# A layer norm's reciprocal square root as a power on GpSimd, tile by tile, with a finer opening and a new order of the early key chunks

## The chip, the cores and the metric

The kernel runs on one core of one Trainium2 chip. The metric is device time in microseconds (us), the median of several executions. Engines by the profile's names: PE is TensorE, PEld its weight loads, DVE is VectorE, ACT is ScalarE, POOL is GpSimd. L-numbers in profile lines are lines of the kernel that was profiled, so the same statement has other numbers before and after.

Ratios are the mean time of one kernel's runs over that of the other's of the same rounds, so not quite the ratio of the medians quoted.

## The reference

One pre-norm block: attention with 32 heads of 16 on 2048 tokens of width 512, then a gated feed-forward of width 1792.

```python
def _layernorm(x, axis=-1, eps=1e-5):
    m = jnp.mean(x, axis=axis, keepdims=True)
    v = jnp.var(x, axis=axis, keepdims=True)
    return (x - m) / jnp.sqrt(v + eps)

h  = x + attention(_layernorm(x))            # q, k, v = norm(x) @ wqkv; softmax; @ wo
h2 = h + (sigmoid(n @ w_gate) * (n @ w_up)) @ w_down     # n = _layernorm(h)
```

## The kernel before

The kernel is recorded by a Python program that keeps its own clock for each engine and lays down a static order of instructions from assumed durations. The attention is 2048 units (one head, 128 keys, 512 queries). ScalarE does most of the exponentials; VectorE does the rest with integer arithmetic (a first pass named `J`, then four-unit passes named `X`). The background work (layer norm, projections, later the feed-forward) is fitted between.

A unit needs its key chunk: 512 keys, normalised, transposed, projected. At the start only chunk 0 exists, so the first units depend on how fast chunks 1 to 3 are made ready. Each group of four heads must have all its value products in one accumulator before the next group's may start, so exponentials of a later group are held in one of 44 slots.

Before, the opening took one square root for four tiles on ScalarE and projected 512 queries at once:

```python
Task(("r", 0), [("f", 0, i) for i in range(TQ)], [("A", 330, lambda: A.activation(
    out=rstds[0][:], in_=mvs[0][:, :, 1], func=ACT.Sqrt, bias=eps_t[:, 0:1]))])
Task(("i", 0), [("r", 0)], [("D", 180, lambda: V.reciprocal(...))])
# ... apply, transpose, copy per tile, then:
Task("k", es + ["w0"], [("P", 1000, lambda: proj0(0))], bank=1)     # 4 matmuls, 128x512
Task("q", es + ["w0"], [("P", 1000, lambda: proj0(1))], bank=1)
```

The later layer norms, all but the last one in the tail, used an integer first guess and two Newton steps on VectorE, eleven small operations, once for a chunk and after the last tile's statistics:

```python
def newton_jobs(dst, var, *dep, pr=0):
    ...
    def seed():                      # 3 operations
        V.tensor_scalar(out=v[:], in0=var, scalar1=1e-5, scalar2=None, op0=ALU.add)
        ...                          # shift, multiply-add on int32
    def step(out):                   # 4 operations, done twice
        V.tensor_tensor(out=t[:], in0=y[:], in1=y[:], op=ALU.mult)
        ...
def early_ln(c):
    ...                              # statistics of 4 tiles -> js
    jn = newton_jobs(rstds[c][:], mvs[c][:, :, 1], *js, pr=pr)
    for i in range(TQ):
        ja.append(dve(325, lambda i=i: apply(c, i), jn, ...))
```

The order of the first blocks, as (group, key chunk), all for query chunk 0:

```python
early = [(0, 0), (0, 1), (1, 0), (0, 2), (0, 3), (1, 1), (1, 2), (1, 3)]
```

## Time and profile before

| | before |
|---|---|
| median (range), us | 837.8 (833.7 to 838.7, 4 runs) |
| span of the profiled run, us | 836.8 |
| first exponential of the attention, us | 16.95 |
| ScalarE busy, 20 to 70 us | 27.3 of 50 |
| eleven-operation chains on VectorE | 8 |

Busy time by engine, and the group of VectorE's exponentials (count, busy us, mean ns), from the page of the kernel before:

```profile
PE 748.3 (89%) x8275; PEld 289.7 (35%) x8275; DVE 779.3 (93%) x1525; ACT 766.8 (92%) x786; POOL 2.9 (0%) x7
...
L1109 DVE TENSOR_SCALAR J<-PS 128x512 int16<-128x512 f32 x470 | 312.4, 684 | 13.6 <-PE PS L986 7.9
```

VectorE and ScalarE are both over 90% busy over the whole span, and that hides the start. The table of windows for 20 to 70 us (us from the span's start, then each engine's busy us and instruction count, then the granted clock and DMA):

```profile
core 0: us, PE busy (x) PEld busy (x) DVE busy (x) ACT busy (x) POOL busy (x), PEclk, DMA share, GB/s
20.00:30.00 10.00, 8.26 (x59) 2.87 (x58) 8.58 (x25) 6.04 (x7) 0.00 (x0) 1.00 0.01 2
30.00:40.00 10.00, 9.31 (x71) 3.25 (x70) 8.82 (x29) 10.00 (x13) 0.00 (x0) 1.00 0.00 0
40.00:50.00 10.00, 7.93 (x25) 1.76 (x24) 5.23 (x9) 4.61 (x6) 0.00 (x0) 0.62 0.00 0
50.00:60.00 10.00, 6.37 (x31) 2.46 (x30) 7.59 (x23) 2.64 (x3) 0.00 (x0) 0.67 0.09 21
60.00:70.00 10.00, 9.23 (x42) 2.24 (x40) 5.50 (x9) 4.03 (x5) 0.00 (x0) 0.68 0.47 165
```

ScalarE falls to 2.64 of 10 us, VectorE too is far from full, and the granted clock is 0.62 to 0.68 on average from 40 to 70 us. ScalarE's waits from 18 to 70 us (total us, times, longest):

```profile
ACT pt L1252 <- PE PS L986: 19.9, 9, 8.4
ACT pe L1252 <- PE PS L986: 2.7, 1, 2.7
```

So 22.6 us are waits for scores. The longest, 8.4 us, stands behind this stretch of VectorE's timeline (start, us, instruction), the chain for chunk 3:

```profile
53.68 0.16 DVE L657 TENSOR_SCALAR nv<-mv 128x4 f32<-128x4 f32 x1
...
55.67 0.16 DVE L668 TENSOR_TENSOR rstd<-ny,nt 128x4 f32<-128x4 f32 x1
55.87 0.41 DVE L334 TENSOR_SCALAR xn_551<-xb_111,mv,rstd 128x512 bf16<-128x512 bf16 x1
```

Eleven operations take 53.68 to 55.87, and only then can the first of four tiles be applied. In the opening (timeline of all engines):

```profile
1.25 2.26 POOL L235 MEMSET Vaug<- 128x512 bf16 x1
...
1.54 2.01 DVE L240 TENSOR_SCALAR ident_76<-ident_bf 128x128 bf16<-128x128 bf16 x1
...
9.64 0.41 DVE L334 TENSOR_SCALAR xn_179<-xb_108,mv,rstd 128x512 bf16<-128x512 bf16 x1
...
12.86 2.98 PE L347 MATMUL PS<-xnT_80,w_114 128*128 128x512 bf16 x8 [0.61 <-DVE xnT_80 L341]
...
16.95 1.94 ACT L1252 ACTIVATE pt<-PS 128x1024 f16<-128x1024 f32 x2 [0.48 <-PE PS L986]
```

The first apply starts at 9.64 us, and the eight projections take 2.98 us. The doubling of a 128x128 identity takes 2.01 us; it ends with GpSimd's memset.

### The profile page before, as it was taken

How to read it: one execution, taken by the hardware profiler on the slowest of the kernel's cores; microseconds unless marked ns; L12 is line 12 of the kernel's file. 1: busy time of each engine (PE TensorE's matmuls, PEld its weight loads, DVE VectorE, ACT ScalarE, POOL GpSimd, SP SyncE). 2: the span in 40 equal slices, each digit the busy share in tenths (PEclk: the TensorE clock that was granted, in tenths of full speed). 3: DMA queues.
4: the chain of work that ended last, by engine and by line, in shares of the span. 5: the costliest groups of instructions: out<-in, count | busy, mean ns of one | idle time of the engine just before them, and what ended most of it. 6: DMA issues, size and time to landing. Idle time of an engine off the chain costs nothing.

```text
span 836.8 us, 19835 instructions
## 1 busy us (share of the span) xinstructions
PE 748.3 (89%) x8275; PEld 289.7 (35%) x8275; DVE 779.3 (93%) x1525; ACT 766.8 (92%) x786; POOL 2.9 (0%) x7
## 2 busy tenths in 40 slices
PE   4879988888989989999998999899989999989987
PEld 1322222222222232222233334333444454344444
DVE  6858999999999999999999999999998999999963
ACT  5728999999999999999899999998998999989952
POOL 1000000000000000000000000000000000000000
PEclk9959999999999999999999999999997999999999
DMA  6010000200000001021000021010211133013050
GB/s 213 1 59 30 1 1 1 65 1 1 2 1 2 14 1 51 26 64 51 20 20 3 27 65 52 27 33 14 71 52 52 40 105 100 14 32 98 8 183 16
DMA packets 53055, 33.83 MB, mean 40 GB/s; under 512 B 3040, under 2 KB 52960, under 8 KB 52960
## 3 DMA queue, kind: packets, MB, share of 16 engines
q1 hardware_dynamic: 51328, 31.33, 12.4%
q8 instruction: 66, 1.08, 0.5%
q10 hardware_dynamic: 1632, 1.18, 0.4%
q14 instruction: 29, 0.24, 0.1%
HBM read 30.41 MB, written 2.10 MB: 39 GB/s over the span
## 4 chain that ended last, share of the span: by engine, by line
ACT 39%; PE 27%; DVE 25%; issue 8%; DMA 1%; SPq 0%; ACTq 0%; DVEq 0%
ACT pt L1252 35%; DVE J L1109 9%; PE PS L986 8%; PE PS L754 5%; PE PS L735 5%; PE PS L1086 4%; DVE X L1143 4%; ACT pe L1252 2%; DVE hT L807 2%; DVE X L1133 2%; ACT th L765 2%; PE PS L270 1%; DVE X L1138 1%; DVE Vaug L274 1%; DVE xs L1034 1%
## 5 line engine op out<-in xcount | busy, mean ns | idle before, releaser
L1252 ACT ACTIVATE pt<-PS 128x1024 f16<-128x1024 f32 (+2 forms) x661 | 706.9, 1253 | 33.8 <-PE PS L986 22.3
L1109 DVE TENSOR_SCALAR J<-PS 128x512 int16<-128x512 f32 x470 | 312.4, 684 | 13.6 <-PE PS L986 7.9
L1086 PE MATMUL PS<-pt,Vaug 128*17 128x256 f16 (+1 forms) x2300 | 176.1, 310 | 1.4 <-DVE xs L1034 0.8
L1143 DVE TENSOR_TENSOR X<-J,X 128x1024 f16<-128x1024 f16 (+1 forms) x244 | 155.9, 665 | 0.0
L1086 PE MATMUL PS<-X,Vaug 128*17 128x256 f16 (+1 forms) x1410 | 139.0, 312 | 4.2 <-DVE X L1133 2.8
L1086 PEld LDWEIGHTS <-Vaug 128*17 128x17 bf16 x3777 | 84.0, 90 | 106.4 <-issue 96.7
L1138 DVE TENSOR_SCALAR X<-J 128x2048 int16<-128x2048 int16 (+2 forms) x127 | 82.0, 645 | 0.1
L1133 DVE TENSOR_SCALAR X<-J 128x2048 int16<-128x2048 int16 (+2 forms) x127 | 82.0, 645 | 0.0
L735 PE MATMUL PS<-xnT_80,wgu 128*128 128x256 bf16 (+1 forms) x336 | 63.5, 320 | 0.9 <-DVE hT L807 0.2
L735 PEld LDWEIGHTS <-wgu 128*128 128x128 bf16 x560 | 46.3, 99 | 45.4 <-issue 30.9
L754 PE MATMUL PS<-wd,hT 128*128 128x512 bf16 x196 | 55.1, 383 | 0.0
L986 PEld LDWEIGHTS <-KT_84 32*128 32x128 bf16 x768 | 23.6, 92 | 80.5 <-issue 74.6
L986 PEld LDWEIGHTS <-KT_85 32*128 32x128 bf16 x768 | 24.9, 92 | 70.7 <-issue 68.7
L549 PE MATMUL PS<-wo_sb 128*128 128x512 bf16 x143 | 47.8, 386 | 0.2 <-DVE KT_85 L630 0.2
L765 ACT ACTIVATE th<-PS 128x512 f32<-128x512 f32 (+1 forms) x63 | 41.0, 651 | 7.4 <-DVE hT L748 7.1
L986 PEld LDWEIGHTS <-KT_86 32*128 32x128 bf16 x768 | 24.4, 91 | 65.5 <-issue 64.2
L986 PE MATMUL PS<-QT_90,KT_85 32*128 32x256 bf16 (+1 forms) x384 | 36.6, 315 | 10.6 <-ACT pt L1252 9.3
L986 PEld LDWEIGHTS <-KT_87 32*128 32x128 bf16 x768 | 23.1, 91 | 63.6 <-issue 62.8
L986 PE MATMUL PS<-QT_91,KT_85 32*128 32x256 bf16 (+1 forms) x384 | 35.9, 312 | 9.0 <-ACT pt L1252 8.1
L986 PE MATMUL PS<-QT_95,KT_87 32*128 32x256 bf16 (+1 forms) x384 | 36.6, 308 | 5.6 <-ACT pt L1252 5.0
L986 PE MATMUL PS<-QT_94,KT_87 32*128 32x256 bf16 (+1 forms) x384 | 36.8, 308 | 4.9 <-ACT pt L1252 4.1
L986 PE MATMUL PS<-QT_92,KT_86 32*128 32x256 bf16 (+1 forms) x384 | 35.5, 308 | 6.3 <-ACT pt L1252 6.0
(209 smaller groups left out, 644.2 us busy)
## 6 DMA issues: line engine op xcount, KB each, us to landing
wgu<-in_B_w_gate_dram SPq DMA_DIRECT2D x35, 256.0 KB, 2.9
wgu<-in_B_w_up_dram SPq DMA_DIRECT2D x35, 256.0 KB, 3.2
out_dram<-ob SPq DMA_DIRECT2D x16, 128.0 KB, 1.7
wd<-in_B_w_down_dram SPq DMA_DIRECT2D x1, 1792.0 KB, 7.3
xr<-in_A_x_dram SPq DMA_DIRECT2D x14, 128.0 KB, 3.3
X<-in_B_w_gate_dram SPq DMA_DIRECT2D x3, 512.0 KB, 3.8
X<-in_B_w_up_dram SPq DMA_DIRECT2D x3, 512.0 KB, 4.8
wv_sb<-in_A_wqkv_dram SPq DMA_DIRECT2D x1, 512.0 KB, 6.8
```

The lines of the kernel that those rows point to most:

```text
L549: nc.tensor.matmul(PS[:, 1 + (st["ring"] + 1) % st["R"], :], lhsT=wo_sb[:, 0, 0:P], rhs=wo_sb[:, 0, :], start=True, stop=True)
L735: nc.tensor.matmul(ps[:, 0:CW[qc]], lhsT=w[:, d, :], rhs=HN[qc][:, d, cols(qc)], start=(d == 0), stop=(d == DC - 1))
L754: nc.tensor.matmul(ps, lhsT=hT[:, f, q:q + P], rhs=wd[:, f, :], start=(f == 0), stop=(f == FC - 1))
L765: nc.scalar.activation(out=th[:, 0:ps.shape[-1]], in_=ps, func=ACT.Tanh, scale=0.5)
L807: nc.vector.scalar_tensor_tensor(out=hT[:, f:f + k, cols(qc)], in0=th[f][:].rearrange("p (k n) -> p k n", k=k), scalar=1.0, in1=ps2.rearra ...
L986: nc.tensor.matmul(pss[:, ui, i * CW[qc]:(i + 1) * CW[qc]], lhsT=KT[g // 2][32 * j:32 * j + 32, k * P:(k + 1) * P], rhs=q[32 * j:32 * j + ...
L1086: nc.tensor.matmul(acc[32 * j:32 * j + VW, 0:w], lhsT=Vaug[:, kt * SPAN[qc] + i, h, :], rhs=un.ap[:, i * w:(i + 1) * w], start=(c + i == 0 ...
L1109: nc.vector.tensor_scalar(out=J[:, k, :], in0=src, scalar1=ZOFF, scalar2=0.0, op0=ALU.add, op1=ALU.max)
L1133: V.tensor_scalar(out=X[:, 0, 0:k, :], in0=J[:, 0:k, :], scalar1=POWER, scalar2=LITTLE, op0=ALU.bitwise_and, op1=ALU.bitwise_or)
L1138: V.tensor_scalar(out=X[:, 1, 0:k, :], in0=J[:, 0:k, :], scalar1=FRACTION, scalar2=HALF, op0=ALU.bitwise_and, op1=ALU.bitwise_or)
L1143: V.tensor_tensor(out=x, in0=J[:, a:b, :].bitcast(FP16), in1=x, op=ALU.mult)
L1252: ex = nc.scalar.activation(out=pt, in_=pss[:, 0:wa, :], func=ACT.Exp, scale=AS)
```

## The change

The intent: take the small chains off VectorE and let each tile go on alone; load one activation table in place of two; project 128 queries at a time, with matmuls that nobody reads keeping TensorE's clock up; and give ScalarE two groups' units for every key chunk that is ready. The core of the diff:

```diff
+    def rstd_of(dst, var, eps=1e-5):
+        v = small.tile([P, 1], FP32, name="nv")
+        nc.gpsimd.tensor_scalar(out=v[:], in0=var, scalar1=eps, scalar2=None, op0=ALU.add)
+        nc.gpsimd.tensor_tensor(out=dst, in0=v[:], in1=power[:], op=ALU.pow)
...
-    nc.gpsimd.memset(Vaug[:, :, :, DH:VW], 0.5)      # was right after make_identity
-    nc.vector.tensor_scalar(out=ident2[:], in0=ident_bf[:], scalar1=2.0, ...)   # now at the end
+    nc.scalar.activation(out=A0[:], in_=eps_t[:], func=ACT.Exp)
...
-    Task("k", es + ["w0"], [("P", 1000, lambda: proj0(0))], bank=1)
+        Task(("r", 0, i), [("f", 0, i)], [("G", 750, lambda i=i: rstd_of(...))])
+        Task(("a", 0, i), [("r", 0, i)], [("D", 340, lambda i=i: apply(0, i))])
+        for w in (1, 0):
+            Task(("p", w, i), [("e", 0, i), "w0"], [("P", 340, lambda w=w, i=i: proj0(w, i))], ...)
...
+    def keep_warm(until):
+        ...
+            E.matmul(PS[:, 4, :], lhsT=fill[:, 0:P], rhs=fill[:], start=True, stop=True)
...
+    nc.gpsimd.memset(Vaug[:, :, :, DH:VW], 0.5)      # now after the opening's four powers
...
-        jn = newton_jobs(rstds[c][:], mvs[c][:, :, 1], *js, pr=pr)
+            j = rstd_job(rstds[c][:, i:i + 1], mvs[c][:, i, 1:2], j)      # one for each tile
...
-    early = [(0, 0), (0, 1), (1, 0), (0, 2), (0, 3), (1, 1), (1, 2), (1, 3)]
+    early = [(0, 0), (1, 0), (0, 1), (1, 1), (0, 2), (0, 3), (1, 2), (1, 3)]
...
         if st["R"] > 1 and wide["i"] == 0 and late(st["R"] - 1):
+            while st["open"] is not None:       # a guard: no ring place is given up half used
+                flush()
+                try_bg(1e9, 1e12)
```

The later layer norm (`wo_ln`) uses the same power for each tile.

## The prediction

> **What bounds the kernel now.** In the long middle the exponentials do: in the table of windows ScalarE is busy 19.8 to 20.0 us of nearly every 20 us between 70 and 380 us, VectorE 19.7 to 20.0; the page gives ScalarE 92%, VectorE 93%. Around 400 to 420 and 560 to 600 us TensorE is full (up to 20.0 of 20) and ScalarE falls to 18.2 to 18.9. The start is different. In the timeline the first exponential starts at 16.95 us; ScalarE then waits 4.0 us for scores of key chunk 1 (24.4 to 28.4), and from 40 to 70 us it is busy only 11.3 of 30 us, VectorE 18.3 of 30, with the granted clock at 0.50 for most of 43 to 66 us. The longest wait there (view of waits) is 8.4 us for scores, behind the layer norm of chunk 3: eleven tiny VectorE operations, 53.7 to 55.9, then apply, transposes, projection. So before 70 us about 40 us of ScalarE time is not exponentials.
>
> **What the change does, costed.**
> 1. Opening. Today ScalarE issues loads to 4.6 us, loads the square-root table (1.28 us), ends its second statistics pass at 9.2, then takes one square root for all four tiles; VectorE applies from 9.64; the projections run eight 128x512 matmuls in 2.98 us (about 0.43 us apart, against 0.22 later). The change loads the exponential table at once, drops the second table load, lets each tile go on alone and projects 128 queries at a time at a warmed clock. The Trainium skill, "TensorE: Matmul & The Clock Gate", Part 1, says that about 3.4 us of sustained work lifts the halved clock; the 0.43 and 0.22 us spacings agree. Leaving out the doubling of the identity also frees VectorE: 2.01 us today, overlapping GpSimd's 2.26 us memset. I estimate the first exponential at 10.5 us: 6 us earlier.
> 2. Reciprocal square roots. Eight chains of eleven operations, 2.2 us each, leave VectorE: 17.5 us. GpSimd gets 26 pairs of tiny instructions, which no view of before times; the schedule assumes 0.8 us a pair. An exponential costs ScalarE about 0.45 us (706.9 us over 1,578 units) and VectorE about 1.36; rebalancing 17.5 us is worth 17.5 x 0.45/1.81, about 4 us.
> 3. Order. Two groups' units on chunk 0 give ScalarE 32 units, about 15 us, before it needs chunk 1. VectorE needs about 9 us for each chunk's preparation without the chain. The waits at 24 and 40 to 70 us should largely go; they hold about 22 us of ScalarE, 12 us of VectorE. If half is recovered, about 10 us. Held exponentials fill 32 of 44 slots, and the forced flushes may take some back.
>
> These sit on the early critical path; ScalarE-bound work afterwards should move forward as a block. The tail from 800 us stays.
>
> **Prediction.** 837.8 - 6 - 4 - 10 = 818 us; 8 in 10: 804 to 831. Faster over 2%: 0.62; within 2%: 0.35; slower: 0.03.
>
> **What would show it.** First exponential at 9.5 to 12 us; ScalarE over 20 of 30 us busy from 40 to 70; no chains of tiny VectorE operations; GpSimd busy about 20 to 30 us; VectorE exponentials up by about 10 from 470; matmuls of the opening near 0.22 us per 512 columns.
>
> **What would make it wrong.** The powers take far over 0.8 us and the in-order VectorE stands in front of apply. The skill, "GPSIMD Engine Reference", section 1, says the two share SBUF interfaces; the 2.01 us operation beside the memset fits. Or slots run out and ScalarE waits for value products; or low TensorE activity still halves the clock at 40 to 66 us, or somewhere new; or the time won early is lost at TensorE-bound stages, leaving 8 to 12 us.

## The result, and the profile after

The changed kernel takes 812.49 us (811.89 to 812.93, 4 runs) against 837.84 us (4 runs) for the kernel before; ratio 0.971, 95% interval 0.968 to 0.974. The profiled spans are 810.3 and 836.8 us: 26.5 us less.

The same page lines, changed kernel:

```profile
PE 737.8 (91%) x8279; PEld 291.4 (36%) x8279; DVE 767.4 (95%) x1437; ACT 761.7 (94%) x779; POOL 31.1 (4%) x67
...
L1134 DVE TENSOR_SCALAR J<-PS 128x512 int16<-128x512 f32 x472 | 312.5, 683 | 8.5 <-PE PS L1011 2.1
```

The chains are gone and GpSimd works 31.1 us, but VectorE's exponentials are 472, where they were 470. The same windows:

```profile
core 0: us, PE busy (x) PEld busy (x) DVE busy (x) ACT busy (x) POOL busy (x), PEclk, DMA share, GB/s
20.00:30.00 10.00, 9.43 (x73) 3.33 (x71) 9.81 (x24) 9.84 (x12) 5.02 (x12) 1.00 0.01 2
30.00:40.00 10.00, 10.00 (x63) 3.27 (x61) 9.69 (x22) 9.58 (x12) 2.37 (x6) 1.00 0.01 2
40.00:50.00 10.00, 9.74 (x73) 3.01 (x73) 9.49 (x19) 9.65 (x10) 0.79 (x2) 1.00 0.04 5
50.00:60.00 10.00, 8.16 (x53) 2.41 (x53) 7.68 (x15) 6.77 (x8) 0.00 (x0) 1.00 0.55 180
60.00:70.00 10.00, 9.73 (x107) 2.64 (x108) 9.68 (x18) 9.64 (x10) 0.00 (x0) 1.00 0.01 2
```

ScalarE is busy 45.5 of 50 us, and the clock is full from 20 to 70 us. Its waits from 18 to 70 us:

```profile
ACT pt L1280 <- PE PS L1011: 3.1, 4, 2.6
ACT pe L1280 <- PE PS L1011: 1.0, 3, 0.5
ACT pe L1280 <- PE PS L1111: 0.4, 1, 0.4
```

They are 4.5 us in place of 22.6. The opening, however, is barely shorter (timeline):

```profile
6.09 0.38 DVE L349 TENSOR_SCALAR xn_182<-xb_110,mv,rstd 128x512 bf16<-128x512 bf16 x1
...
6.39 0.41 DVE L349 TENSOR_SCALAR xn_184<-xb_110,mv,rstd 128x512 bf16<-128x512 bf16 x1
...
7.73 2.26 POOL L468 MEMSET Vaug<- 128x512 bf16 x1
...
7.81 2.33 DVE L349 TENSOR_SCALAR xn_219<-xb_110,mv,rstd 128x512 bf16<-128x512 bf16 x1 [0.46 <-POOL rstd L260]
...
15.24 2.93 ACT L1280 ACTIVATE pt<-PS 128x1024 f16<-128x1024 f32 x3
```

The first exponential comes at 15.24 us. One apply took 0.41 us, the fourth 2.33; it ends just after GpSimd's memset does (7.73 + 2.26 = 9.99 us). The chain of waits of the changed kernel (start, us, what) shows what else stood in the way:

```profile
4.31 0.23 POOL nv L259
...
7.19 0.60 POOL rstd L260
...
7.81 0.24 DVE xn_219 L349
8.05 2.02 issue
```

The chain runs through GpSimd from the first pair at 4.31 us to the fourth power: four pairs, one after the other, 3.5 us. Then come 0.24 us of the apply and 2.02 us called "issue": this profile shows no event for what held the apply, so the part of it that nothing explains is put there.

**Where the time came from.** A landmark that both kernels pass in the same order is the transposition of a finished group's accumulator (48 in all, read from the timelines). The third starts at 122.2 us before and at 102.5 after: 19.7 us ahead. The lead is 16.3 us at the 32nd (612.6 and 596.3), and 26.1 at the last (804.9 and 778.8). One landmark is not a fine measure: the lead at the first four is 16.7, 21.0, 19.7 and 16.4 us. So 16 to 20 us come from the first 100 us or so, nothing clear is won over the next 500, and the rest is won after 600 us.

### The profile page after: what moved, and what is told of

Its sections match the earlier page's. It is cut to its first block, busy times and chain, and to the rows that moved or that the text cites. A ratio compares the mean times of both kernels' runs of the same rounds, so it can differ in the third digit from the quotient of the medians.

```text
span 810.3 us, 19793 instructions
## 1 busy us (share of the span) xinstructions
PE 737.8 (91%) x8279; PEld 291.4 (36%) x8279; DVE 767.4 (95%) x1437; ACT 761.7 (94%) x779; POOL 31.1 (4%) x67
## 4 chain that ended last, share of the span: by engine, by line
ACT 40%; DVE 25%; PE 23%; issue 10%; POOL 1%; DMA 0%; DVEq 0%; ACTq 0%
ACT pt L1280 36%; DVE J L1134 10%; PE PS L1011 7%; DVE X L1168 5%; PE PS L1111 4%; PE PS L779 4%; PE PS L760 4%; ACT pe L1280 3%; DVE X L1158 2%; DVE hT L832 2%; DVE X L1163 2%; PE PS L284 1%; ACT th L790 1%; DVE xs L1059 1%; PE PS L1418 1%
## 5 line engine op out<-in xcount | busy, mean ns | idle before, releaser
L1280 ACT ACTIVATE pt<-PS 128x1024 f16<-128x1024 f32 (+2 forms) x649 | 689.3, 1238 | 12.5 <-PE PS L1111 6.8
L1163 DVE TENSOR_SCALAR X<-J 128x2048 int16<-128x2048 int16 (+3 forms) x125 | 81.8, 655 | 0.0
L1158 DVE TENSOR_SCALAR X<-J 128x2048 int16<-128x2048 int16 (+3 forms) x125 | 81.7, 654 | 0.0
L1280 ACT ACTIVATE pe<-PS 128x1024 f16<-128x1024 f32 (+2 forms) x44 | 48.0, 1184 | 1.4 <-PE PS L1011 1.0
```

The source lines that it names most:

```text
L1158: V.tensor_scalar(out=X[:, 0, 0:k, :], in0=J[:, 0:k, :], scalar1=POWER, scalar2=LITTLE, op0=ALU.bitwise_and, op1=ALU.bitwise_or)
L1163: V.tensor_scalar(out=X[:, 1, 0:k, :], in0=J[:, 0:k, :], scalar1=FRACTION, scalar2=HALF, op0=ALU.bitwise_and, op1=ALU.bitwise_or)
L1280: ex = nc.scalar.activation(out=pt, in_=pss[:, 0:wa, :], func=ACT.Exp, scale=AS)
```

## The experiments

Three parts can be switched: the opening (O), the power on GpSimd after the opening (R), and the order with its guard (G). For reading, here are all runs in one table. "Wait" is what ScalarE's exponentials waited from 18 to 70 us, "third" the landmark named above, "rest" the span less it, "lead" how much earlier than in the kernel before the first four landmarks come, on average. The lead is the steadier of the two early measures, since each version has its own static order and single landmarks shift by some us with it. Medians are of 4 runs; the kernel before was run 7 times in each of three later sets, with medians of 837.8, 836.5 and 837.0. Each part brings its planned durations along (in R, for instance, 870 ns in place of 810 for one tile's statistics).

| kernel | first exp. | wait | lead | third | rest | span | median |
|---|---|---|---|---|---|---|---|
| before | 16.95 | 22.6 | 0 | 122.2 | 714.6 | 836.8 | 837.8 |
| O alone | 15.44 | 24.0 | -0.5 | 124.6 | 719.9 | 844.5 | 845.7 |
| R alone | 17.54 | 9.0 | 12.2 | 106.0 | 728.1 | 834.1 | 838.0 |
| G alone | 18.25 | 12.4 | 6.6 | 111.1 | 728.4 | 839.5 | 841.3 |
| O and R, mended | 15.74 | 14.0 | 4.1 | 118.3 | 714.6 | 832.9 | 834.3 |
| O and G | 14.89 | 12.9 | 7.6 | 114.6 | 717.1 | 831.7 | 836.2 |
| R and G | 17.07 | 5.3 | 17.5 | 103.3 | 717.9 | 821.2 | 822.9 |
| all: the changed kernel | 15.24 | 4.5 | 18.5 | 102.5 | 707.8 | 810.3 | 812.5 |
| all, chain in later layer norm | 15.24 | 4.5 | 18.5 | 102.5 | 719.6 | 822.1 | 823.4 |
| all, one power for a chunk | 14.98 | 7.8 | 14.2 | 109.9 | 709.4 | 819.3 | 825.8 |
| all, no unread matmuls | 15.70 | 5.8 | 16.3 | 104.5 | 706.6 | 811.1 | 813.4 |
| all, plan's latency 70 ns | 14.91 | 5.6 | 18.0 | 105.8 | 712.0 | 817.8 | 818.9 |
| all, memset first | 12.75 | 4.7 | 20.7 | 100.2 | 708.2 | 808.4 | 810.2 |

### The order alone (g_only)

```diff
-    early = [(0, 0), (0, 1), (1, 0), (0, 2), (0, 3), (1, 1), (1, 2), (1, 3)]
+    early = [(0, 0), (1, 0), (0, 1), (1, 1), (0, 2), (0, 3), (1, 2), (1, 3)]
+            while st["open"] is not None: flush(); try_bg(1e9, 1e12)
```

> The kernel before with the new order of the early blocks alone. Theory 1 (the order is the main part: two groups' units on one key chunk bridge ScalarE's wait for the next chunk): 12 to 16 us faster than before, ScalarE busy over 20 of the 30 us from 40 to 70. Theory 2 (the early hole is made by the eleven-operation chains on VectorE and the halved clock behind them; the order matters little without the power on GpSimd): under 6 us faster, ScalarE under 16 of 30 us there, and the clock still halved between 40 and 70.

Measured: 841.29 us, ratio to before 1.0045 (1.0006 to 1.0085). Theory 1 as I had put it falls: the order alone makes nothing faster. Theory 2's clock condition fails too: the low clock from 40 to 70 us shrinks to one window of 3.4 us at 48.5 us. ScalarE's waits from 18 to 70 us in this run:

```profile
ACT pt L1255 <- PE PS L986: 7.4, 6, 3.1
ACT pe L1255 <- PE PS L1086: 3.2, 2, 1.9
ACT pe L1255 <- PE PS L986: 1.8, 4, 0.9
```

They are 12.4 us, about half of what they were, and 19.8 of the 30 us from 40 to 70 are busy, between the marks of the two theories. The order does bridge part of the hole: the lead over the first four landmarks is 6.6 us. By the end it has been lost again, and why was not tested.

### The power alone (r_only)

```diff
-    jn = newton_jobs(rstds[c][:], mvs[c][:, :, 1], *js, pr=pr)
+        j = rstd_job(rstds[c][:, i:i + 1], mvs[c][:, i, 1:2], j)     # and the same in wo_ln
```

> The kernel before with the power on GpSimd in the early chunks and in the later layer norm alone. Theory 1: 3 to 5 us faster (17.5 us of VectorE work shared out), the wait for chunk 3 at 53 to 62 us stays. Theory 2: 10 us or more faster, the halved clock at 43 to 66 us gone.

Measured: 838.04 us, ratio 1.0023 (0.9975 to 1.0071): nothing. Theory 2's sign is there (no low clock in the records before 285 us; wait 9.0 us, lead 12.2 us), its time is not. The lead is given back between 106 and 430 us, in windows such as these of the same run:

```profile
280.00:300.00 20.00, 15.42 (x108) 5.25 (x108) 16.03 (x32) 14.17 (x14) 3.54 (x6) 0.74 0.00 1
380.00:400.00 20.00, 17.30 (x124) 5.27 (x124) 19.90 (x35) 15.69 (x16) 0.00 (x0) 1.00 0.11 34
```

ScalarE has 14.17 and 15.69 of 20 us there. From 100 to 430 us it waits 14.1 us in this run, 8.8 of them for value products that have to free an exponential's slot; the kernel before waits 3.2 us in that stretch. At 285.3 us the clock was halved for 10.2 us. The 10.9 us more of waits are about what the lead was. Why this static order has them there was not tested.

### The opening alone (o_only)

```diff
# the changed opening; old order, no guard; newton_jobs in early_ln and wo_ln
```

> The new opening alone (loads, one table, tile by tile, 128 queries at a time, unread matmuls, GpSimd power in the first chunk only), old order, chains on VectorE after it. Both theories: first exponential at about 15.2 us as in the changed kernel, against 16.95, so about 2 us faster in all, and no more, because the hole at 40 to 70 us stays. A result of 6 us or more would say that the opening moves the clock's low windows too.

Measured: 845.73 us, ratio 1.0108 (1.0066 to 1.0149): slower, clear of the noise though by under 2%. Neither theory expected that. The first exponential came at 15.44 us, as expected, but the hole stayed (24.0 us of waits), so the earlier start only made ScalarE wait earlier; the clock records hold half clock for 55.1 us in all, against 40.1 before. Why 8 us were lost, and not just nothing won, is not shown.

### Power and order (r_g)

> Power and order together, old opening. If the three parts add up, this is the changed kernel less 2 us: 22 to 25 us faster than before. If the new opening matters more than its 1.7 us (through the warm clock or the earlier start), it is under 20 us faster.

Measured: 822.93 us, ratio 0.983 (0.980 to 0.987), with the two edits above together. It is 14.8 us faster than before, so by the expectation's own mark (under 20 us) the opening counted for more than its 1.7 us. By the third landmark this run is within 0.8 us of the changed kernel; the other 10.1 us come later, where the two kernels have the same work.

Two parts that alone gave +0.3 and +3.5 us give -14.8 together. The table shows where this comes from, and it is not the start: the leads of R and G alone, 12.2 and 6.6 us, add up to about the 17.5 us of both. It is what follows. At the end of the span R alone is 2.7 us ahead of the kernel before and G alone 2.7 behind, so each has lost over 9 us of its lead; both together are 15.6 ahead and have lost 1.9. So these three runs don't show that the two parts need each other in the first 100 us; they show that each alone loses its lead later, for a reason that stays open.

### Without the order: a wrong result (o_r), and mended (o_r_mended)

> The changed kernel with the old order of early blocks. So far: order alone 841.3, power alone 838.0, opening alone 845.7, power and order 822.9, all three 812.5. Theory A (order and power need each other: the order gives ScalarE 32 units to chew, the power makes VectorE deliver the next chunk before they are eaten, so either alone leaves the hole): 830 to 838, with ScalarE idle for 8 us or more in 20 to 50 us. Theory B (each part's worth is only the luck of the static plan that the recording makes): anything from 812 to 845, unrelated to the early idle time.

This version was the changed kernel with the old order and without the guard. It gave a wrong result (relative error 0.24; 834.78 us), which shows what the guard is for; its time is not used. The two single-part runs without the guard (R alone and O alone) were correct.

```diff
-    early = [(0, 0), (1, 0), (0, 1), (1, 1), (0, 2), (0, 3), (1, 2), (1, 3)]
+    early = [(0, 0), (0, 1), (1, 0), (0, 2), (0, 3), (1, 1), (1, 2), (1, 3)]
     # the guard stays
```

> The run without the new order once more, with the guard that keeps a ring place from being given up while a background item is half done in it (its absence gave the wrong result). Theory A (order and power need each other) expects 830 to 838 us again and ScalarE idle for 8 us or more between 20 and 50 us; if the wrong run's time was an artefact of its wrong plan, 812 to 822.

Measured: 834.30 us, ratio 0.9955 (0.991 to 1.000), correct, 14.0 us of waits. The time is where theory A put it: without the order, the power and the opening are worth under 1%. The other sign is weaker than expected: ScalarE was idle for 6.5 us between 20 and 50 us, not for 8 or more. The lead is 4.1 us.

### Without the power (o_g)

```diff
-            j = rstd_job(rstds[c][:, i:i + 1], mvs[c][:, i, 1:2], j)
+        jn = newton_jobs(rstds[c][:], mvs[c][:, :, 1], *js, pr=pr)           # and in wo_ln
```

> The changed kernel with the eleven-operation chain on VectorE again in the early chunks and in the later layer norm (the power stays in the first chunk). Theory A: 830 to 840, the wait for chunk 3 near 45 to 60 us is back as in the run of the order alone (ScalarE busy under 15 of 20 us there). Theory B: no relation.

Measured: 836.23 us, ratio 1.0003 (0.998 to 1.003), waits 12.9 us. The time is again where theory A put it: the order and the opening without the power are worth nothing. ScalarE was busy 11.8 of 20 us from 40 to 60, as expected. The lead is 7.6 us. With the new opening, then, the two parts do need each other at the start: with one of them the lead is 4.1 or 7.6 us, with both 18.5.

### The chain back in the later layer norm alone (wo_newton)

```diff
-            jr.append(rstd_job(rstd[:, i:i + 1], mv[:, i, 1:2], j))
+        jn = newton_jobs(rstd[:, 0:n], mv[:, 0:n, 1], j)
```

> The changed kernel with the chain back in the later layer norm alone; early chunks keep the power. If freeing VectorE in the long middle is worth what the prediction says (five chains of 2.2 us, 11 us of VectorE, times 0.25), 814 to 817 us; if the middle gives nothing (its landmarks showed none between 100 and 600 us), 811 to 814; over 820 would say that the later chains cost more than their VectorE time, through low clock windows.

Measured: 823.38 us, ratio 0.984 (0.982 to 0.987). It equals the changed kernel within 0.1 us for the first ten landmarks (up to 254 us), is then up to 5.6 us ahead of it (at 382 us), and after that falls behind, to 10.3 us at the last. That is more than either of my smaller figures. Low clock does not explain it: the clock is at half for 10.2 us from 428 us, where the changed kernel has 3.4 us, but over the whole span it is at half for 18.6 us, less than the changed kernel's 20.7. Read this one with the run after next.

### One power for a whole chunk (pool_whole)

```diff
-            j = rstd_job(rstds[c][:, i:i + 1], mvs[c][:, i, 1:2], j)         # each tile
+        j = rstd_job(rstds[c][:], mvs[c][:, :, 1], *ja)                      # after the last tile
```

> The changed kernel with the power still on GpSimd, but after the opening one pair of instructions for a whole chunk after its last statistics, instead of one pair for each tile. It takes as much off VectorE as the change does. If the worth of the power is that it frees VectorE, 811 to 816 us; if it is that each tile's apply and transposes go on alone, without waiting for the last tile's statistics, 820 us or more, with waits of ScalarE for scores back between 25 and 60 us.

Measured: 825.77 us (820.2 to 831.7), ratio 0.989 (0.982 to 0.996). Two runs lie near 821 us and two near 831, the latter at a mean clock of 0.967 and 0.971 against 0.987 and 0.989; the profile is of one of the faster. VectorE is freed as in the change, and the time is still higher. ScalarE's waits from 18 to 70 us:

```profile
ACT pe L1283 <- PE PS L1114: 2.5, 2, 1.7
ACT pt L1283 <- PE PS L1014: 2.4, 4, 1.4
ACT pt L1283 <- PE PS L1114: 1.7, 2, 0.9
ACT pe L1283 <- PE PS L1014: 1.2, 4, 0.4
```

The time fits the second reading, that going on tile by tile is part of the worth. Its sign did not come: the waits for scores (L1014) are 3.6 us, no more than the 4.1 of the changed kernel, and what is new are 4.2 us of waits for value products (L1114). The lead is 14.2 us against 18.5. So this run does not tell the two readings apart, and the next one adds to the doubt.

### A plan made with another assumption (lat_70)

```diff
-    LAT = 60.0
+    LAT = 70.0
```

> A change with no meaning to the chip: the plan's assumed latency of a hand-over is 70 instead of 60 ns, so the static order comes out differently after the first few microseconds. It measures how far a plan alone moves the time, with the same work. If the parts measured so far stand well clear of that, under 4 us from 812.5; if theory B (luck of the plan) carries a good part of the 10 us steps, 817 us or more.

Measured: 818.91 us (817.6 to 822.8), ratio 0.980 (0.976 to 0.983). No work changed, and the time is 6.4 us higher. It falls in my second range (817 us or more): the luck of the plan can carry a good part of a 10 us step. The lead is 18.0 us, close to the 18.5 of the changed kernel, so most of the loss comes later; single landmarks shift both ways (the second is 2.3 us earlier than in the changed kernel, the third 3.3 us later). It is one sample, but it sets a scale: a difference of 6 us between two of these plans can't be put down to the edited part, and where another plan would fall isn't known. The 22 and 24 us that are lost when the order or the power is taken away are more than three times that; the 14.8 us of power and order together are a little over twice. The size of the later layer norm's share (10.9 us) and of the tile-by-tile share (13.3 us, with a wide interval) is not settled.

### Without the unread matmuls (no_fill)

```diff
-            E.matmul(PS[:, 4, :], lhsT=fill[:, 0:P], rhs=fill[:], start=True, stop=True)
             free["P"] += ns
```

> The changed kernel without the unread matmuls of the opening. If they keep the clock up where it counts, the opening's transposes and projections go at 0.43 us per 512 columns, the first exponential comes 1 to 2 us later and the time rises to 813.5 to 815; [...]I rather expect under 1 us of difference, 812 to 813.5.

Measured: 813.43 us, ratio 0.972 (0.969 to 0.975). The first exponential came at 15.70 us, 0.46 later. The landmarks come 2.0 to 2.7 us later than in the changed kernel up to 254 us, and 0.6 at the end; the runs of the two overlap (811.5 to 814.3 and 811.9 to 812.9). So the unread matmuls are worth about half a us in the opening, where the clock of the changed kernel was at half from 11.4 to 14.9 us anyway, just when the projections ran: twelve 128-column matmuls in 1.44 us, 0.43 us apart when scaled to 512 columns. TensorE had little to do from 8 to 10.5 us while VectorE's apply was held. They help more just after it: without them the 512-column matmuls at 15.6 to 17.7 us are still 0.43 us apart, where the changed kernel's are 0.22.

### The memset first (memset_first)

```diff
     make_identity(nc, ident_bf[:])
+    nc.gpsimd.memset(Vaug[:, :, :, DH:VW], 0.5)
...
-    nc.gpsimd.memset(Vaug[:, :, :, DH:VW], 0.5)       # after the opening's powers
     free["G"] += 2300                                  # kept, so the plan stays the same
```

> The changed kernel with GpSimd's 2.26 us memset of the ones columns put right after the identity, where VectorE waits for loads, instead of after the fourth power; the plan's numbers untouched, so every other instruction stands as before. If the memset holds up VectorE's fourth apply through the shared interface (2.33 us against 0.41 for its three sisters), that apply falls to 0.41, the first exponential comes at 13.3 instead of 15.2 us, and the time falls by 1 to 2 us to about 811. If the apply was long for another reason, nothing moves.

Measured: 810.24 us (809.5 to 810.8), ratio to before 0.969 (0.967 to 0.972), the fastest version. Its timeline:

```profile
1.25 2.27 POOL L245 MEMSET Vaug<- 128x512 bf16 x1
...
1.68 1.86 DVE L250 TENSOR_SCALAR maskz<-mask 128x2 f32<-128x2 f32 x1
...
7.91 0.41 DVE L350 TENSOR_SCALAR xn<-xb,mv,rstd 128x512 bf16<-128x512 bf16 x1 [0.46 <-POOL rstd L261]
...
12.75 1.94 ACT L1280 ACTIVATE pt<-PS 128x1024 f16<-128x1024 f32 x2
```

The fourth apply is back at 0.41 us and the first exponential comes at 12.75 us. The blocked one is now another VectorE instruction, the scaling of a 128x2 mask: 1.86 us against 0.17 in the changed kernel, again ending as the memset ends, but at a time when VectorE has little else to do (its first statistics start at 3.41 us, 3.31 in the changed kernel). The apply is shorter by 1.92 us and the first exponential comes 2.49 us earlier; the projections also ran at full clock here (twelve in 0.83 us, 1.44 in the changed kernel), and this run does not separate the two. All 45 landmarks from the fourth on are earlier by 1.8 to 2.0 us than in the changed kernel: here the plan is the same, and a gain in the opening moves the whole run forward as a block. The runs of the two kernels (809.5 to 810.8 and 811.9 to 812.9) don't overlap, though they were not taken in the same set.

## Why the prediction was right

The time was right: 818 us predicted, 804 to 831, and 812.5 measured; the direction and the place of most of the gain too. The terms of the sum were not, and that they came out so near is in part luck: some 8 us too much for the opening and the rebalancing stand against some 7 too little for the hole and the last 10 us, which were not foreseen.

1. **The hole at 20 to 70 us.** Right: it was where most of the gain lay, ScalarE was busy 26.1 of the 30 us from 40 to 70 (11.3 before), the low clock there went, and the held exponentials in 32 of 44 slots did no visible harm. The term, "about 10 us" for the order, was mis-sized: the lead over the first four landmarks is 18.5 us, of which the earlier first exponential is 1.7. And it is not the order's alone. O and G without R end at 836.2 us and O and R without G at 834.3, both about where the kernel before is; all three bring 812.5. My explanation, that the order gives ScalarE units to work on while the power gets the next chunk ready before they are used up, fits these two (waits of 12.9 and 14.0 us against 4.5). It is argued, not shown: with the old opening the leads of the two parts simply add.
2. **"6 us earlier" for the opening.** This step failed: 1.7 us. The experiment shows 1.8 to 2.5 us of the difference: the change moved GpSimd's memset to where VectorE's fourth apply runs. I had used the old overlap (2.01 us) as a gain for taking the doubling away, and had not asked where the memset would go. Taking it away won nothing: the first statistics start at 3.31 us, and started at 3.23 before. The timelines show where the lead went. At the first apply the changed kernel is 3.55 us ahead (6.09 against 9.64); at the start of the fourth 2.81, since the applies now come at the pace of the GpSimd pairs (3.5 us for four in a row); at its end 0.89, since it was held; at the first exponential 1.71. I had listed a slow power only as a risk. The halved clock under the projections is a further part, whose size was not tested by itself.
3. **"Rebalancing 17.5 us is worth about 4."** The chains left as told, but the rebalancing didn't take place: VectorE's exponentials went from 470 to 472, not up by 10. (In R alone they did rise, to 482, and no time was won.) The worth of the power shows at the start (point 1); whether it is there the earlier apply of each tile or VectorE's freed time is not settled. Some of it may lie in the later layer norm, with a size between nothing and the 10.9 us of the run, given what a plan alone can move.
4. **"Should move forward as a block."** True where the plan stays the same (memset first), false between plans: R alone was 16.2 us ahead at 106 us and had 2.7 us left at the end of the span. I had named this loss at later stages as a risk, at TensorE-bound ones; what the run showed are waits for value products and scores, and a low clock window at 285 us. Even with one plan a gain need not stay whole: the 2.7 us between the runs with and without the unread matmuls at 254 us were 0.6 at the end.
5. **The last 10 us**, between 613 and 805 us, I had not predicted at all. The kernel before has the clock at half for 3.4 us from 622.7 and 10.2 us from 636.3, with ScalarE busy 35.8 of 40 us from 620 to 660; the changed one has none between 428 and 776 us, and 39.1 of 40. That they cause it was not tested by itself, and R alone had 6.8 us of half clock from 626.7 us as well. An estimate from runs with the plan of the changed kernel speaks against it as the whole cause: across places where the run without unread matmuls has one low window of 3.4 us more or less than the changed kernel, it lost 0.7 us or made good 0.8 and 1.2, and the run with the memset first lost 0.6 us across a window of 6.8; at these rates 13.7 us of half clock cost about 1 to 5 us. This stays open; so does why the middle of R alone, G alone and O alone ran slower than that of the kernel before.

The Trainium skill, "TensorE: Matmul & The Clock Gate", Part 1, says the clock gate looks at a free-running window of 3413 ns. The trace agrees: the clock records of these runs hold half clock for 3.4, 6.8 or 10.2 us. It fits, too, that the same fifteen unread matmuls, from 1.5 us on in both, came to full speed at about 4.6 us in the changed kernel and at about 6.2 us in the run with the memset first.

The Trainium skill, "SBUF — State Buffer", "SBUF: two separate sides", says that GpSimd and a VectorE instruction that needs the shared port pair exclude each other for a whole instruction. The trace agrees three times: 2.01, 2.33 and 1.86 us for VectorE instructions that end 0.02 to 0.15 us after the memset beside them.

## What to carry to other kernels

Two parts that each leave the time unchanged can together be worth a good deal, so try them together before dropping one; and look at where each alone stands along the way, since here both led early (by 12.2 and 6.6 us) and lost it later. When work leaves a busy engine for an idle one, ask what else on the idle engine shares a resource with it, and move that to a time when nobody minds. Measure first how far a neutral change of the static plan moves the time; smaller steps than that say nothing about their cause, unless the plan is held fixed.

## What the Trainium skill lacked or had wrong

- "GPSIMD Engine Reference" has no duration for a power. In the changed kernel's trace it took a median of 569 ns on 128x1 in float32 (568 to 1321, 30 times), the addition before it 223 ns (218 to 1025), and pairs in a row started 0.86 us apart.
- "SBUF — State Buffer" describes the lock but not how a profile shows it: as one long VectorE instruction (2.33 us against 0.41 for a sister), whose held part the chain of waits calls "issue" (2.02 us), with no wait recorded against the memset. Even an instruction on 128x2 elements was held (1.86 us against 0.17).
- "TensorE: Matmul & The Clock Gate" says in Part 1 that the point of warming up varies by 500 ns either way from run to run; between two runs with the same matmuls from 1.5 us on it came about 1.6 us apart (4.6 and 6.2 us). The same part also tells of 6, 11 or 14 slow matmuls for one kernel; in these two runs 7 and 11 of them were spaced 0.43 us, which lies in that range.
- "TensorE: Matmul & The Clock Gate" warns in Part 1 against trusting single clock events. Neither it nor another page that I read says that the view of the clock used here reads full before its first record (15.1 us in the kernel before): there it reads 1.00 from 10 to 20 us while the opening's matmuls are 0.43 us apart, twice the 0.22 us seen later.
